# One stretch of fixed order from the second phase on, and attention's round in six steps

## The chip, the cores and the metric

The kernel runs on one core of one Trainium2 chip. The metric is the device time of one execution in microseconds, the median of several runs. TensorE (PE, with its weight loads as PEld), VectorE (DVE), ScalarE (ACT) and GpSimd (POOL) work beside each other; each takes its own instructions in order, and semaphores hold an instruction until its inputs are there and its output's buffer is free. SyncE (SP) issues all DMAs of this kernel, in one queue.

## The reference

Three layers follow each other on 4 x 768 = 3072 tokens of 256 values. A decayed linear attention (8 heads of 32 values, a state of 16 x 32 a head) goes over the sequence in chunks:

```
M = (C B^T) * exp(cum_i - cum_j), causal
y = M x + (C state) * exp(cum)
state = exp(sum) * state + sum_j B_j x_j * exp(cum_end - cum_j)
```

A first feed-forward layer takes `h = max(x w1, x w2, x w3)` (256 to 768) and `h w_out` (768 to 256); a second takes `h = x w_in` (256 to 2048), `g = max(h, 0) + alpha * min(h, 0)` and `g w_out`. The weights come as 64-bit floats.

## The kernel before

**Tiles.** The feed-forward layers run on six tiles of 512 tokens. Every operand is kept as two float32r halves, high and low, and a product is three matmuls (high by high, low by high, high by low). A unit of the first layer is 128 columns of `h`: three ups of six matmuls (`up<-xt,w`), ScalarE's copy `g<-up` of the first, VectorE's maximum with the two others, the halves `gh` (ScalarE) and `gl` (GpSimd, `halves`), and two units later a down of six matmuls (`acc<-gh,wo`, `acc<-gl,wo`). A unit of the second layer is one up of six (`up<-yt,vi`), two VectorE operations (a `TENSOR_SCALAR` and a `SCALAR_TENSOR_TENSOR` to `g`), the same halves, and a down with `vo`. `up` has 3 buffers of PSUM, `acc` 2, attention's `at` 3. At a layer's end `end1` writes `yt` from `acc` with ScalarE and VectorE.

**Phases.** PHASES lists (layer, tile): first layer on tile 0 (in two halves), first layer on tile 1, second layer on tile 0, first layer on tile 2, second layer on tile 1, and so on to two last phases of the second layer. The first layer has 6 units a tile, the second 16. In what follows the phases are counted from one; the second phase is the first layer on tile 1, from 83 us on, and the third the second layer on tile 0, from 121.7 us on. The two downs that are left of a phase are carried into the next (`carry`).

**Attention** goes block by block (24 blocks of 128 tokens, `r`), four blocks for each tile. Its steps are `load`, `att_a` (GpSimd: B and C times decays), `att_t` (transposes), `att_e` (exponentials on ScalarE, then the causal select on GpSimd), `att_b` (the product of C and B, `at<-bc` or `at<-st,v`, and VectorE's multiplication into `e`), `att_u` (the state), `att_y` (the output, `at<-cpt,u` and `at<-e,xm`, then `xt` by ScalarE and VectorE). From block 12 on (NDIR) the blocks are wide: `att_s` writes `tok`, VectorE transposes it to `ts`, `att_t` writes that to DRAM (`sc`), and `att_l` reads it back in eight DMAs to `v` and `st` buffers. `rounds` strings the steps together; a round is five of them. `quota` says how many steps are due after a unit, `attend` takes the next one.

**Weights.** 28 pieces of weights are converted on the way: a DMA to one of three `st` buffers, a re-bias on ScalarE (`st<-st`), a shift and an or on VectorE (`v<-st`, `v<-st,v`), a copy on ScalarE (`vi<-v`) and a subtract on VectorE (`vi<-v,vi`). `slot` and `quota_w` pace them.

**What sets the order.** In the first three phases the scheduler of the tile framework sets each engine's order. From `n_ph >= STRICT` (3, the fourth phase) on, every phase is a stretch in which instructions stand as they are written (`tc.manual_schedule`); there attention's steps are taken after an up and after a down.

Of the kernel before, what the change touches and what calls it, by code (L numbers as in the profile page):

```python
# [37 lines left out]

LEADW = 12288

STRICT = 3
AHEAD = 10
START = 4
LAG = 2
NX = 3

# [31 lines left out]
def fused(ctx: ExitStack, tc: tile.TileContext, x, a, B, C, w1, w2, w3, w_out, v_in, v_out, alpha, cst, out):  # L78
# [133 lines left out]
    def load(r):  # L212
        for q in (r, r + 1)[r > AHEAD:1 + (r >= AHEAD)]:
            load_bc(q)
        load_x(r)
# [210 lines left out]
        nc.scalar.activation(blk[r]["m"], src, AF.Exp)  # L426
        yield

    def att_e(r):
        b, k = divmod(r, NB)  # L430
        if r >= NDIR:
            for g in range(2):
                e = blk[r]["m", g]
                for q in range(4):
                    nc.scalar.activation(e[:, q, :], e[:, q, :], AF.Exp, bias=ncum[:, k, b, 4 * g + q:4 * g + q + 1])  # L435
                nc.gpsimd.affine_select(out=e, in_=e, pattern=[[0, 4], [1, P]], compare_op=ALU.is_ge, fill=0.0, base=0, channel_multiplier=-1)  # L436
            return
        e = blk[r]["m"]
        for h in range(H):
            nc.scalar.activation(e[:, h, :], e[:, h, :], AF.Exp, bias=ncum[:, k, b, h:h + 1])  # L440
        for c in range(2):
            m = e[c * Q:(c + 1) * Q]
            nc.gpsimd.affine_select(out=m, in_=m, pattern=[[0, H], [1, Q]], compare_op=ALU.is_ge, fill=0.0, base=0, channel_multiplier=-1)  # L443

# [112 lines left out]
    def rounds(r0):  # L557

        for r in range(r0, NR):
            if r + 2 < NR:  # L560
                yield lambda r=r: att_a(r + 2), 0
            yield lambda r=r: (att_y(r), r + 1 < NR and att_u(r + 1)), r + 1
            if r + 2 < NR:
                late = r + 2 == NDIR
                yield lambda r=r, late=late: (att_e(r + 1), late or att_s(r + 2)), 0
                yield lambda r=r, late=late: (att_b(r + 1), att_s(r + 2) if late else att_t(r + 2)), 0
                yield lambda r=r, late=late: (late and att_t(r + 2), load(r + 3), att_l(r + 2)), 0
            elif r + 1 < NR:
                yield lambda r=r: att_e(r + 1), 0
                yield lambda r=r: att_b(r + 1), 0  # L570

    todo = []
    y_done = [0]
# [53 lines left out]
    def halves(g, n, engine=nc.gpsimd):  # L627
# [2 lines left out]
        split(gh[:, :n], gl[:, :n], g, engine)  # L630
        return gh[:, :n], gl[:, :n]

    def up1(ph, f, o, n):
        t = ph[1]
        fs = slice(f * P, (f + 1) * P)
        g = un.tile([P, 512], F32, tag="g", name="g")[:, :n]
        for j in range(3):
            need(4 * (f // 2) + j)
            p = up_mm([w[:, j, :, fs] for w in w123], xt[t], o, n)
            if j == 0:  # L640
                nc.scalar.activation(g, p, AF.Copy)  # L641
            else:
                nc.vector.tensor_tensor(g, p, g, ALU.max)  # L643
            slot()
        return halves(g, n)

    def up2(ph, f, o, n):
        t = ph[1]
# [133 lines left out]
    if True:  # L782
# [10 lines left out]
        plan = [u for ph in PHASES for u in units_of(ph)]  # L793

        owed, at = 0.0, 0
        for n_ph, ph in enumerate(PHASES):
            with tc.manual_schedule() if n_ph >= STRICT else nullcontext():
                layer, t, _, pace = ph
                up, end = (up1, end1) if layer == 1 else (up2, end2)
                pend = []  # L800
                for f, o, n, _, blocks, _ in units_of(ph):
                    until(blocks)
                    owing[1] = pace or quota_w(at)
                    if n_ph >= STRICT and layer == 2 and len(pend) == 1:
                        carry.pop(0)()
                    pend.append((f, o, n, up(ph, f, o, n)))
                    owed += quota(at)
                    at += 1
                    while n_ph >= STRICT and owed > 0.999 and todo:
                        owed -= 1  # L810
                        attend()
                    if carry:
                        carry.pop(0)()
                    elif tail:
                        tail.pop(0)()
                    if len(pend) > LAG:
                        down(ph, *pend.pop(0))
                    slot()
                    if layer == 2:
                        slot()  # L820
                    while owed > 0.999 and todo:
                        owed -= 1
                        attend()
                for i, u in enumerate(pend):
                    def go(ph=ph, u=u, finish=end if i == LAG - 1 else None):
                        down(ph, *u)
                        if finish:
                            finish(ph)
                    carry.append(go)
        with tc.manual_schedule():  # L830
            for u in pend[:-1]:
                down(ph, *u)
            f, _, _, g = pend[-1]
            for o, n in LAST:
                down(ph, f, o, n, [x[:, o:o + n] for x in g])
                end2_last(ph, o, n)
                while tail:
                    tail.pop(0)()


_INS = ['x', 'a', 'B', 'C', 'moe_w1', 'moe_w2', 'moe_w3', 'moe_w_out', 'moe2_w_in', 'moe2_w_out', 'moe2_alpha']
# [22 lines left out]
```

## Time and profile before

| | us |
|---|---|
| runs: median of 3 | 553.9 |
| runs: lowest, highest | 553.26, 555.51 |
| the profiled execution | 553.52 |
| its span, first to last instruction | 551.8 |
| busy in the span: PE | 536.2 |
| busy: DVE, ACT, POOL | 330.5, 221.6, 235.0 |

The busy time of PE is modelled, since matmuls overlap: an engine at 97% may still wait. The chain of work that ended last is what sets the end, and the places where PE sat idle are what an order can change. The granted clock of TensorE is that of the full level (2.4 GHz) in every slice of the page.

### The profile page before, as it was taken

Reading aid. Unit: us, or ns where it says so; the run is one execution under the profiler, and the core shown is the slowest. Engines: PE = TensorE matmul, PEld = TensorE weight load, DVE = VectorE, ACT = ScalarE, POOL = GpSimd, SP = SyncE. Lnnn points to the kernel's source line nnn. Section 1 sums busy time; section 2 is a strip of 40 time slices with the busy share of each in tenths; the row PEclk is TensorE's granted clock in tenths of the full one; section 3 lists DMA queues with packets and bytes.
Section 4 is the critical chain, followed back from the end, with each engine's and each line's share of the span. In section 5 each row is a group of like instructions: output and inputs, shape, how many; then the busy total and the mean of one; then the engine's idle time right before and its main releaser. Section 6 shows DMA issues by size and latency. Waiting matters only on the chain.

```text
span 551.8 us, 9739 instructions
## 1 busy us (share of the span) xinstructions
PE 536.2 (97%) x3541; PEld 432.4 (78%) x3542; DVE 330.5 (60%) x587; ACT 221.6 (40%) x556; POOL 235.0 (43%) x256
## 2 busy tenths in 40 slices
PE   8888999999999999999999999999999999999996
PEld 4667888767878888788788788888777888888885
DVE  5887898986565446665446665446654326556553
ACT  5667687863232244244244244233342222222222
POOL 2143445454453245564235555333643214444441
PEclk9999999999999999999999999999999999999999
DMA  7978779731123853743773634743420200002001
GB/s 146 229 149 182 193 171 214 227 78 28 30 40 80 155 97 90 152 70 85 128 114 95 131 65 111 124 93 87 67 63 2 38 1 0 1 0 39 0 2 39
DMA packets 185632, 49.84 MB, mean 90 GB/s; under 512 B 144112, under 2 KB 177072, under 8 KB 185584
## 3 DMA queue, kind: packets, MB, share of 16 engines
q1 hardware_dynamic: 185584, 49.22, 42.4%
q8 instruction: 28, 0.46, 0.4%
q14 instruction: 20, 0.16, 0.1%
HBM read 40.48 MB, written 8.72 MB: 89 GB/s over the span
## 4 chain that ended last, share of the span: by engine, by line
PE 77%; DVE 7%; ACT 4%; DMA 4%; issue 3%; SPq 2%; POOL 1%; ACTq 0%; DVEq 0%; POOLq 0%
PE up L619 41%; PE acc L619 29%; DVE v L171 2%; PE at L523 1%; ACT e L440 1%; DMA st<-in_moe_w_out_dram 1%; DVE g L643 1%; PE at L452 1%; POOL gl L130 1%; DMA st<-in_moe_w_in_dram 1%; DMA e<-cum_w 1%; DMA e<-cum_d 1%; DVE e L467 1%; PE at L520 1%; ACT st L162 1%
## 5 line engine op out<-in xcount | busy, mean ns | idle before, releaser
L130 POOL TENSOR_TENSOR gl<-g,gh 128x512 fp32r<-128x512 f32 (+1 forms) x137 | 172.6, 1260 | 257.1 <-ACT gh L129 242.6
L129 ACT ACTIVATE gh<-g 128x512 fp32r<-128x512 f32 (+1 forms) x138 | 84.5, 612 | 261.7 <-DVE g L654 184.0
L619 PE MATMUL up<-xt,w 128*128 128x512 f32 (+1 forms) x756 | 161.5, 363 | 2.5 <-ACT g L641 1.7
L619 PEld LDWEIGHTS up<-xt,w 128*128 128x128 f32 x756 | 128.5, 188 | 27.6 <-ACT g L641 2.4
L619 PE MATMUL up<-yt,vi 128*128 128x512 f32 x576 | 146.0, 390 | 0.0
L619 PEld LDWEIGHTS up<-yt,vi 128*128 128x128 f32 x576 | 107.7, 188 | 23.0 <-issue 0.4
L653 DVE TENSOR_SCALAR g<-up,alph 128x512 f32<-128x512 f32 x96 | 71.8, 748 | 85.4 <-PE up L619 77.1
L619 PE MATMUL acc<-gh,vo 128*128 128x512 f32 (+1 forms) x392 | 120.5, 389 | 0.6 <-DVE yt L682 0.6
L643 DVE TENSOR_TENSOR g<-up,g 128x512 f32<-128x512 f32 (+1 forms) x84 | 51.4, 611 | 71.0 <-PE up L619 61.2
L619 PEld LDWEIGHTS acc<-gh,vo 128*128 128x128 f32 x392 | 72.1, 188 | 15.5 <-DVE yt L682 1.1
L619 PE MATMUL acc<-gl,vo 128*128 128x512 f32 (+1 forms) x196 | 76.0, 388 | 1.0 <-POOL gl L130 0.8
L654 DVE SCALAR_TENSOR_TENSOR g<-up,g 128x512 f32<-128x512 f32 x96 | 66.3, 691 | 3.3
L619 PE MATMUL acc<-gh,wo 128*128 128x512 f32 (+1 forms) x168 | 47.3, 366 | 0.2 <-ACT gh L129 0.2
L619 PEld LDWEIGHTS acc<-gl,vo 128*128 128x128 f32 x196 | 36.8, 188 | 9.9 <-POOL gl L130 2.1
L619 PEld LDWEIGHTS acc<-gh,wo 128*128 128x128 f32 x168 | 29.5, 189 | 5.7 <-ACT gh L129 0.4
L641 ACT ACTIVATE g<-up 128x512 f32<-128x512 f32 (+1 forms) x42 | 22.3, 532 | 26.2 <-PE up L619 15.9
L435 ACT ACTIVATE e<-e,ncum 128x128 f32<-128x128 f32 x96 | 29.6, 388 | 4.5 <-DMA e<-cum_w 4.5
L619 PE MATMUL acc<-gl,wo 128*128 128x512 f32 (+1 forms) x84 | 30.2, 360 | 0.0
L443 POOL TENSOR_SCALAR_AFFINE_SELECT e<-e 64x512 f32<-64x512 f32 x20 | 17.1, 856 | 14.9 <-ACT e L440 14.1
L440 ACT ACTIVATE e<-e,ncum 128x64 f32<-128x64 f32 x80 | 21.9, 341 | 2.3 <-DMA e<-cum_d 2.3
L171 DVE SCALAR_TENSOR_TENSOR v<-st,v 128x512 uint32<-128x512 uint32 x28 | 21.9, 783 | 0.9 <-ACT st L162 0.3
L454 DVE TENSOR_TENSOR e<-at,e 128x512 f32<-128x512 f32 x24 | 16.0, 686 | 10.4 <-POOL e L436 10.4
(123 smaller groups left out, 396.9 us busy)
## 6 DMA issues: line engine op xcount, KB each, us to landing
e<-cum_w SPq DMA_DIRECT2D x24, 256.0 KB, 4.4
st<-sc SPq DMA_DIRECT2D x48, 128.0 KB, 3.0
st<-in_moe_w_out_dram SPq DMA_DIRECT2D x11, 512.0 KB, 5.2
st<-in_moe_w_dram SPq DMA_DIRECT2D x9, 512.0 KB, 5.0
sc<-ts SPq DMA_DIRECT2D x40, 112.0 KB, 3.0
st<-in_moe_w_in_dram SPq DMA_DIRECT2D x8, 512.0 KB, 4.5
v<-sc SPq DMA_DIRECT2D x48, 64.0 KB, 2.8
out_dram<-st SPq DMA_DIRECT2D x22, 128.0 KB, 3.3
```

Of the source, the lines that this page charges most:

```text
L129: nc.scalar.activation(dst_h, src, AF.Copy)
L130: engine.tensor_tensor(dst_l, src, dst_h, ALU.subtract)
L171: nc.vector.scalar_tensor_tensor(v, hi, 3, v, ALU.logical_shift_left, ALU.bitwise_or)
L435: nc.scalar.activation(e[:, q, :], e[:, q, :], AF.Exp, bias=ncum[:, k, b, 4 * g + q:4 * g + q + 1])
L440: nc.scalar.activation(e[:, h, :], e[:, h, :], AF.Exp, bias=ncum[:, k, b, h:h + 1])
L443: nc.gpsimd.affine_select(out=m, in_=m, pattern=[[0, H], [1, Q]], compare_op=ALU.is_ge, fill=0.0, base=0, channel_multiplier=-1)
L454: nc.vector.tensor_tensor(ef, cb, ef, ALU.mult)
L619: nc.tensor.matmul(acc, w, r, start=(first and i == 0), stop=(last and i == len(todo_) - 1), skip_group_check=True)
L641: nc.scalar.activation(g, p, AF.Copy)
L643: nc.vector.tensor_tensor(g, p, g, ALU.max)
L653: nc.vector.tensor_scalar(g, p, 0.0, alph[:, f:f + 1], ALU.min, ALU.mult)
L654: nc.vector.scalar_tensor_tensor(g, p, 0.0, g, ALU.max, ALU.add)
```

## The change

- STRICT becomes 1: one single stretch of fixed order reaches from the second phase to the end, and only the first phase is left to the scheduler.
- In such phases the first layer's steps of attention are also handed out inside a unit, after its second up (`within`), and half of a unit's due steps count before the unit.
- From block 6 on (FINE) `rounds` calls `fine`, a round in six steps. The exponentials come in two halves (`att_e(r, part)`): the first half of block r + 2 at the end of round r, the second at the start of round r + 1, each with its select. `att_y`, `att_b`, `att_t` and `att_l` are steps of their own in wide blocks, and `att_l` stands ahead of `load`. In the one round where the wide blocks begin (`late`), the product of block 11 stands ahead of the output of block 10.
- AHEAD becomes 8 for 10: B and C are loaded a block ahead from block 8 on.
- The `gl` of the last unit of the first layer (not on tile 0) is made by VectorE.

```diff
-STRICT = 3
-AHEAD = 10
+STRICT = 1
+AHEAD = 8
+FINE = 6
...
-                yield lambda r=r, late=late: (late and att_t(r + 2), load(r + 3), att_l(r + 2)), 0
+                yield lambda r=r, late=late: (late and att_t(r + 2), att_l(r + 2), load(r + 3)), 0
...
+    def fine(r):
+        more, near = r + 2 < NR, r + 1 < NR
+        late = r + 2 == NDIR
+        if near:
+            yield lambda: (more and att_a(r + 2), att_e(r + 1, 1 if r > FINE else None)), 0
+        if late:
+            yield lambda: (att_b(r + 1), att_s(r + 2)), 0
+        yield lambda: (att_y(r), near and att_u(r + 1), more and not late and att_s(r + 2)), r + 1
+        if near and not late:
+            yield lambda: (att_b(r + 1), r + 2 < NDIR and att_t(r + 2)), 0
+        if more and r + 2 >= NDIR:
+            yield lambda: att_t(r + 2), 0
+            yield lambda: att_l(r + 2), 0
+        if more:
+            yield lambda: (load(r + 3), att_e(r + 2, 0)), 0
...
             slot()
-        return halves(g, n)
+            if j == 1 and within:
+                within[0]()
+        return halves(g, n, nc.vector if t and f == NF1 - 1 else nc.gpsimd)
...
-            with tc.manual_schedule() if n_ph >= STRICT else nullcontext():
...
+            if n_ph == STRICT:
+                fixed.enter_context(tc.manual_schedule())
+                within.append(hand_out)
...
+                own = quota(at)
+                if n_ph >= STRICT and layer == 1:
+                    owed += own / 2
+                    own /= 2
```

Three places of the new order follow. The first is VectorE in the middle of the second phase, where `v`, `vi` and `vo` belong to weights, `g<-up` to the feed-forward layer and `u`, `xt`, `e`, `bc` to attention. Before:

```order
L171 SCALAR_TENSOR_TENSOR v<-st,v 128x512
L169 TENSOR_SCALAR v<-st 128x512
L171 SCALAR_TENSOR_TENSOR v<-st,v 128x512
L554 TENSOR_TENSOR xt_1691<-at,xt_1690 128x128 x2
L501 TENSOR_TENSOR u<-at,ct 128x128
L177 TENSOR_TENSOR vi_114<-v,vi_113 128x2x256
L507 SCALAR_TENSOR_TENSOR u<-u,dec_f 128x64
L177 TENSOR_TENSOR vo_116<-v,vo_115 128x512
L507 SCALAR_TENSOR_TENSOR u<-u,dec_f 128x64
L169 TENSOR_SCALAR v<-st 128x512
L643 TENSOR_TENSOR g<-up,g 128x512
L171 SCALAR_TENSOR_TENSOR v<-st,v 128x512
```

Now:

```order
L171 TENSOR_SCALAR v<-st 128x512
L173 SCALAR_TENSOR_TENSOR v<-st,v 128x512
L666 TENSOR_TENSOR g<-up,g 128x512 x2
L179 TENSOR_TENSOR vo_116<-v,vo_115 128x512
L556 TENSOR_TENSOR xt_1630<-at,xt_1629 128x128 x2
L503 TENSOR_TENSOR u<-at,ct 128x128
L509 SCALAR_TENSOR_TENSOR u<-u,dec_f 128x64 x2
L171 TENSOR_SCALAR v<-st 128x512
L173 SCALAR_TENSOR_TENSOR v<-st,v 128x512
L666 TENSOR_TENSOR g<-up,g 128x512 x2
L179 TENSOR_TENSOR vi_114<-v,vi_113 128x2x256
L469 TENSOR_TENSOR e<-at,e 128x256 x2
```

Before, ten rows stand ahead of the next maximum `g`: attention's, and parts of four pieces of weights. Now six rows, with parts of two pieces, stand between two pairs of maxima.

The second is the start of the third phase on PE, where `up<-yt,vi` is the second layer, `acc<-gh,wo` a carried down of the first, and `at<-bc` the product of block 10 (before) or 11 (now). Before:

```order
L619 MATMUL up<-yt_1607,vi_113 128x512 x2
L619 MATMUL up<-yt_1607,vi_114 128x512 x2
L619 MATMUL up<-yt_1608,vi_113 128x512 x2
L619 MATMUL acc<-gh,vo_115 128x512
L619 MATMUL acc<-gh,vo_116 128x512
L619 MATMUL acc<-gl,vo_115 128x512
L619 MATMUL acc<-gh,vo_115 128x512
L619 MATMUL acc<-gh,vo_116 128x512
L619 MATMUL acc<-gl,vo_115 128x512
L462 MATMUL at<-bc 64x128 x8
```

Now:

```order
L640 MATMUL up<-yt_1667,vi_113 128x512 x2
L640 MATMUL up<-yt_1667,vi_114 128x512 x2
L640 MATMUL up<-yt_1668,vi_113 128x512 x2
L464 MATMUL at<-bc 64x128 x8
L640 MATMUL up<-yt_1667,vi_113 128x512 x2
L640 MATMUL up<-yt_1667,vi_114 128x512 x2
L640 MATMUL up<-yt_1668,vi_113 128x512 x2
L538 MATMUL at<-cpt,u 64x64 x8
L546 MATMUL at<-e,xm_106 32x64 x16
L497 MATMUL at<-xm_107,bp 32x128 x4
L640 MATMUL acc<-gh,vo_115 128x512
```

The first down of the second layer came right after the carried ones and one up; now two ups, the product of block 11 and the output of block 10 (`at<-cpt,u`, `at<-e,xm`) stand ahead of it. VectorE at the same place, before:

```order
L653 TENSOR_SCALAR g<-up,alph 128x512
L654 SCALAR_TENSOR_TENSOR g<-up,g 128x512
L682 TENSOR_TENSOR yt_1968<-acc,yt_1967 128x512 x2
L653 TENSOR_SCALAR g<-up,alph 128x512
L654 SCALAR_TENSOR_TENSOR g<-up,g 128x512
L467 TENSOR_TENSOR e<-at,e 128x256 x2
L393 TENSOR_TENSOR bc<-at,ct 128x256
L653 TENSOR_SCALAR g<-up,alph 128x512
```

Now:

```order
L678 TENSOR_SCALAR g<-up,alph 128x512
L679 SCALAR_TENSOR_TENSOR g<-up,g 128x512
L173 SCALAR_TENSOR_TENSOR v<-st,v 128x512
L707 TENSOR_TENSOR yt_2003<-acc,yt_2002 128x512 x2
L678 TENSOR_SCALAR g<-up,alph 128x512
L679 SCALAR_TENSOR_TENSOR g<-up,g 128x512
L179 TENSOR_TENSOR vi_114<-v,vi_113 128x2x256
L469 TENSOR_TENSOR e<-at,e 128x256 x2
L356 MEMSET tok 128x768
L171 TENSOR_SCALAR v<-st 128x512
```

A piece's rows (`v<-st,v`, `vi<-v,vi`) stand among the second layer's `g`, and the first `e` comes behind one of them.

The third is ScalarE in two rounds of wide blocks inside a phase of the second layer. Before:

```order
L129 ACTIVATE gh<-g 128x512
L435 ACTIVATE e<-e,ncum 128x128 x8
L363 ACTIVATE tok<-b 128x128
L364 ACTIVATE tok<-c 128x2x4x16
L129 ACTIVATE gh<-g 128x512 x5
L553 ACTIVATE xt_2634<-at 128x128 x2
L129 ACTIVATE gh<-g 128x512 x2
L435 ACTIVATE e<-e,ncum 128x128 x8
```

Now:

```order
L131 ACTIVATE gh<-g 128x512
L437 ACTIVATE e<-e,ncum 128x128 x4
L131 ACTIVATE gh<-g 128x512
L437 ACTIVATE e<-e,ncum 128x128 x4
L131 ACTIVATE gh<-g 128x512
L555 ACTIVATE xt_2555<-at 128x128 x2
L365 ACTIVATE tok<-b 128x128
L366 ACTIVATE tok<-c 128x2x4x16
```

Eight exponentials (`e<-e,ncum`) stood in one row; now they stand in two rows of four with a `gh` between, and the output's `xt` behind them.

## Rows read from the trace of the kernel before

**Rows 1.** The page: the chain that ended last, shares of the span by engine.

```profile
PE 77%; DVE 7%; ACT 4%; DMA 4%; issue 3%; SPq 2%; POOL 1%; ACTq 0%; DVEq 0%; POOLq 0%
```

**Rows 2.** Timeline of a steady stretch: start us, us, engine, line, operation [idle before].

```profile
147.08 1.52 PE L619 MATMUL up<-yt,vi 128*128 128x512 f32 x6
148.44 0.61 PE L619 MATMUL acc<-gh,vo 128*128 128x512 f32 x2
...
151.37 1.29 POOL L130 TENSOR_TENSOR gl<-g,gh 128x512 fp32r<-128x512 f32 x1 [1.83 <-PE up L619]
...
152.61 0.65 PE L462 MATMUL at<-bc 64*64 64x128 f32 x14
```

**Rows 3.** PE's waits from 83 us on: us in total, times, longest us.

```profile
PE acc L619 <- POOL gl L130: 0.8, 2, 0.4
...
PE at L452 <- DMA st<-sc: 0.4, 1, 0.4
```

**Rows 4.** Timeline, the end of the second phase, PE and ACT.

```profile
112.77 0.39 PE L619 MATMUL acc<-gl,wo 128*128 128x512 f32 x1
...
113.20 0.67 ACT L162 ACTIVATE st<-st 128x512 f32<-128x512 f32 x1 [0.36 <-DMA st<-in_moe_w_out_dram]
...
114.39 3.88 PE L619 MATMUL up<-xt,w 128*128 128x512 f32 x14 [1.24 <-ACT g L641]
...
119.03 0.62 PE L619 MATMUL acc<-gh,wo 128*128 128x512 f32 x2
```

**Rows 5.** Timeline, the start of the third phase, PE and DVE.

```profile
127.27 1.52 PE L619 MATMUL up<-yt,vi 128*128 128x512 f32 x6
...
128.68 1.29 DVE L682 TENSOR_TENSOR yt<-acc,yt 128x512 fp32r<-128x512 f32 x2 [1.02 <-ACT yt L681]
...
129.43 0.73 PE L619 MATMUL acc<-gh,vo 128*128 128x512 f32 x2 [0.63 <-DVE yt L682]
```

**Rows 6.** Timeline at 222 us, DVE and PE.

```profile
216.76 0.69 DVE L454 TENSOR_TENSOR e<-at,e 128x512 f32<-128x512 f32 x1 [1.34 <-POOL e L436]
...
222.37 0.61 PE L619 MATMUL acc<-gh,vo 128*128 128x512 f32 x2
...
223.40 0.50 PE L619 MATMUL acc<-gl,vo 128*128 128x512 f32 x1 [0.42 <-POOL gl L130]
...
223.74 0.62 PE L619 MATMUL acc<-gh,vo 128*128 128x512 f32 x2
```

**Rows 7.** Stretches: length, then busy (instructions) of PE, PEld, DVE, ACT, POOL; clock; DMA.

```profile
83.00:121.70 38.70, 37.34 (x297) 28.95 (x295) 33.96 (x61) 29.66 (x75) 20.73 (x20) 1.00 0.70 180
121.70:168.50 46.80, 46.17 (x332) 36.68 (x329) 29.52 (x52) 13.57 (x32) 22.01 (x23) 1.00 0.23 41
```

**Rows 8.** Groups in the second phase, then the third: shapes xcount | busy us, mean ns | idle.

```profile
L171 DVE SCALAR_TENSOR_TENSOR v<-st,v 128x512 uint32<-128x512 uint32 x11 | 8.4, 760 | 0.4 <-ACT st L162 0.3
...
L169 DVE TENSOR_SCALAR v<-st 128x512 uint32<-128x512 uint32 x10 | 6.0, 596 | 0.9 <-DMA st<-in_moe_w_in_dram 0.9
...
L177 DVE TENSOR_TENSOR vo<-v,vo 128x512 fp32r<-128x512 f32 x6 | 4.4, 742 | 1.4 <-ACT vo L175 1.3
...
L467 DVE TENSOR_TENSOR e<-at,e 128x256 f32<-128x256 f32 x4 | 1.5, 410 | 0.0
...
L130 POOL TENSOR_TENSOR gl<-g,gh 128x512 fp32r<-128x512 f32 x6 | 9.5, 1579 | 8.0 <-ACT gh L129 7.9
...
L130 POOL TENSOR_TENSOR gl<-g,gh 128x512 fp32r<-128x512 f32 x15 | 19.3, 1290 | 21.3 <-ACT gh L129 17.8 <-PE up L619 1.8 <-PE at L544 1.4
...
L653 DVE TENSOR_SCALAR g<-up,alph 128x512 f32<-128x512 f32 x15 | 11.2, 749 | 11.8 <-PE up L619 11.6
```

**Rows 9.** Timeline, an output of the first layer's phases, PE and DVE.

```profile
270.64 0.64 PE L523 MATMUL at<-e,xm 128*32 128x128 f32 x16
...
271.93 0.49 DVE L554 TENSOR_TENSOR xt<-at,xt 128x128 fp32r<-128x128 f32 x2 [0.86 <-ACT xt L553]
```

**Rows 10.** PE's waits from 20 to 83 us.

```profile
PE at L462 <- DVE xt L554: 1.1, 1, 1.1
```

More of the change, by code (lines that the diff above doesn't have):

```diff
@@ L427, in first_e, with att_e @@
         yield
-    def att_e(r):
+    def att_e(r, part=None):
         b, k = divmod(r, NB)
         if r >= NDIR:
-            for g in range(2):
+            for g in range(2) if part is None else (part,):
                 e = blk[r]["m", g]
@@ L438, in att_e @@
         e = blk[r]["m"]
-        for h in range(H):
+        for h in range(4 * (part or 0), 4 if part == 0 else H):
             nc.scalar.activation(e[:, h, :], e[:, h, :], AF.Exp, bias=ncum[:, k, b, h:h + 1])
-        for c in range(2):
+        for c in range(0 if part == 0 else 2):
             m = e[c * Q:(c + 1) * Q]
@@ L559, in rounds @@
         for r in range(r0, NR):
+            if r >= FINE:
+                yield from fine(r)
+                continue
             if r + 2 < NR:
@@ L631, in halves @@
         return gh[:, :n], gl[:, :n]
+    within = []
     def up1(ph, f, o, n):
@@ L795, in fused @@
         owed, at = 0.0, 0
-        for n_ph, ph in enumerate(PHASES):
-            with tc.manual_schedule() if n_ph >= STRICT else nullcontext():
[L798 to L817, printed above, removed]
-                    slot()
[L819 to L838, printed above, removed]
+        fixed = ExitStack()
+        def hand_out():
+            nonlocal owed
+            while owed > 0.999 and todo:
+                owed -= 1
+                attend()
@@ new lines, in fused, with go @@
+        for n_ph, ph in enumerate(PHASES):
+            if n_ph == STRICT:
+                fixed.enter_context(tc.manual_schedule())
+                within.append(hand_out)
+            layer, t, _, pace = ph
+            up, end = (up1, end1) if layer == 1 else (up2, end2)
+            pend = []
+            for f, o, n, _, blocks, _ in units_of(ph):
+                until(blocks)
+                owing[1] = pace or quota_w(at)
+                own = quota(at)
+                if n_ph >= STRICT and layer == 1:
+                    owed += own / 2
+                    own /= 2
+                if n_ph >= STRICT and layer == 2 and len(pend) == 1:
+                    carry.pop(0)()
+                pend.append((f, o, n, up(ph, f, o, n)))
+                owed += own
+                at += 1
+                if n_ph >= STRICT:
+                    hand_out()
+                if carry:
+                    carry.pop(0)()
+                elif tail:
+                    tail.pop(0)()
+                if len(pend) > LAG:
+                    down(ph, *pend.pop(0))
+                slot()
+                if layer == 2:
+                    slot()
+                hand_out()
+            for i, u in enumerate(pend):
+                def go(ph=ph, u=u, finish=end if i == LAG - 1 else None):
+                    down(ph, *u)
+                    if finish:
+                        finish(ph)
+                carry.append(go)
@@ L841 @@
+        for u in pend[:-1]:
+            down(ph, *u)
+        f, _, _, g = pend[-1]
+        for o, n in LAST:
+            down(ph, f, o, n, [x[:, o:o + n] for x in g])
+            end2_last(ph, o, n)
+            while tail:
+                tail.pop(0)()
+        fixed.close()
 _INS = ['x', 'a', 'B', 'C', 'moe_w1', 'moe_w2', 'moe_w3', 'moe_w_out', 'moe2_w_in', 'moe2_w_out', 'moe2_alpha']
```

## The prediction

> **What bounds the kernel now.** I read the chain of work first: three quarters of it is PE, so PE's own row of matmuls sets the end, and other engines matter only where they make PE wait [rows 1]. Then the steady stretch of the second layer: six matmuls of 512 columns start every 1.36 us (147.08 to 148.44), 0.227 us each, and a 512-column feed-forward matmul cannot come sooner anywhere in this kernel [rows 2]. The change adds and takes away no matmul, and PE has 33 groups of attention matmuls between feed-forward ones from the second phase on, where it had 34 (one moves ahead into the first phase). So PE's work stands, and only its waits can go or come.
>
> The list of PE's waits from 83 us on, where the second phase begins, is short [rows 3], and each place is seen in the timeline. Times below are from start to start, less 0.227 us a matmul; after each stop the first matmul also takes 0.11 us longer.
> - Second phase, 112.77 to 119.03 us: 1.62 - 0.23 = 1.39 us, in which PE waits for ScalarE's copy `g`, queued behind a `st` that waits for a weight's DMA; then 18 matmuls take 4.64 us where 18 x 0.227 = 4.08, 0.56 more. Together 1.95 us [rows 4].
> - Border to the third phase: the first `acc<-gh,vo` starts 2.16 us after six matmuls began that need 1.36: 0.80 us, waiting for VectorE's `yt` [rows 5].
> - Two equal places (222 and 306 us) of 0.58 + 0.11 us: `gl` comes late, since VectorE's queue stood 1.34 us at `e`, waiting for GpSimd's select after eight exponentials in a row [rows 6]. Together 1.38 us.
> - One wait of 0.43 us for `st<-sc` (389 us) [rows 3].
> The sum is 1.95 + 0.80 + 1.38 + 0.43 = 4.56 us. That is all there is to gain after the first phase.
>
> **Weights spread out.** In the second phase VectorE is busy 34.0 of 38.7 us and in the next 29.5 of 46.8 [rows 7]. The crowd is the conversion of weights: 11 pieces, each 0.60 + 0.76 + 0.74 = 2.1 us on VectorE [rows 8]. By the new order 5 stand in the second phase and 6 in the third, so 6 x 2.1 = 12.6 us move: 34.0 becomes 21.4 of 38.7, and 29.5 becomes 42.1 of 46.8. Each piece is also issued with its DMA two to three pieces ahead, at a piece in a unit of 24 x 0.227 = 5.4 us instead of one in 38.7 / 11 = 3.5, so `st` on ScalarE no longer meets a DMA in flight. I count the 1.95 us as gone. What is late next there is PE itself: VectorE has 17 us to spare.
>
> **The border and the exponentials.** The last unit's `gl` goes to VectorE (some 0.74 us, as the subtract of a piece, which has the same size, against GpSimd's 1.29 us [rows 8]), both trailing downs are put ahead of the next up, and two ups and the attention work lie between them and the first `acc<-gh,vo`: some 5 us where `yt` needs 1.29 [rows 5]. The 0.80 us go. With the exponentials done in halves, two steps ahead of the product that reads them, VectorE finds the select done: the 1.38 us go. The reads `st<-sc` get a step of their own right behind the transposes and ahead of the loads, a whole round before their matmul: the 0.43 us go. On SP these eight reads pass three loads, which are wanted a round later; nobody waits for those.
>
> **What it adds.** (1) At the start of the third phase the product of block 11 stands before block 10's output, one up apart (the PE rows of the change). Both take two of the three `at` buffers, so the second half of the output must wait until VectorE's first `e` has read the product. From the end of the last trailing down: `yt` needs about 0.8 for PE's tail and ScalarE's first copy (its second half is ready as soon as VectorE is) and 1.29 on VectorE, `g` of the next up 2 x 0.75 (its second operation taken as long as the first), the `vi` piece 0.74, the first `e` 0.41: 4.7 us [rows 5, 8]. PE comes there after an up, eight pairs and an up: 1.36 + 0.65 + 1.36 = 3.4 us [rows 2]. I take 4.7 - 3.4 = 1.3, with the piece's copy ahead of `yt` on ScalarE 1.5 us, plus 0.11 us: 1.6 us. Bounds: 0, if `yt` and the piece come a unit sooner, and 2.5 us, if two steps of VectorE also meet GpSimd's `gl`. Queued behind it on PE are only downs, whose halves are ready.
> (2) The six pieces in the third phase push `gl` back. In the steady stretch the `gl` of the up at 147.08 us ends at 152.66 [rows 2]. It is the third matmul of the down that stands five sixes later: 147.08 + 5 x 1.36 + 2 x 0.227 = 154.33, so 1.7 us of slack. A shift and an or of one piece are 1.36 us, which fits; with a product (2 x 0.41) or a transpose behind it, it does not. Two or three of 12 units are so placed; half a wait of 0.69 us [rows 6] is 0.35 us, bounds 0 and 6 x 0.69 = 4.1 us.
> GpSimd's own durations speak to this: `gl` takes 1.58 us among conversions and 1.29 without [rows 8]. The Trainium skill (SBUF — State Buffer, "Who interferes with whom") says that a VectorE instruction with two SBUF inputs and a GpSimd instruction that reads SBUF shut each other out for a whole instruction; the rows agree. By the row 0.29 us comes off a slack of 1.7 and the sum stands; by the rule's worst, a whole `or` and a whole `subtract` in the way of one `gl`, 1.5 us come off it, and every piece costs a wait. By the row the sum is 550.9, by the rule 554.6, the rival B below.
> (3) In three places later on the product follows the output by only six matmuls. There `xt` is done 1.78 us after the output's first matmul with `e` (270.64 to 272.42), and the product comes 0.64 + 1.36 = 2.0 us after it [rows 9]: no wait, with 0.2 us to spare; at most three waits of 0.4.
> (4) In the first phase the scheduler now sees that phase alone: a pair of pieces fewer is drawn into it, a product more. PE's order there is nearly the same. I take 0; bounds -1.1 and +1.1 us, the largest single wait there [rows 10].
>
> **The sum**, against the profiled execution (553.5 us, span 551.8): 553.5 - 4.56 + 1.6 + 0.35 = 550.9 us. The median of the runs is 553.9, 0.4 above it; their spread is 2.2 us.
>
> **The rivals.**
> A, the forecast: 550.9, between 549.3 (no wait of kind 1) and 552.5. Chance 0.50.
> B, the conversions bite in the third phase: VectorE and GpSimd take turns, and each of six pieces costs one wait of 0.69 us: 553.5 - 4.56 + 1.6 + 4.1 = 554.6. For it: VectorE at 42 of 47 us, crowded into 12 of 16 units, and `gl` at 1.58. Against it: the second phase had 11 pieces in 38.7 us and lost 1.95 us. Chance 0.22.
> C, slower, by one transfer: block 12's reads `st<-sc` take a place in the ring of three `st` buffers that the weights use. They wait in SP's order for the write of `sc` and for a piece to be read, and the last weight's DMA stands behind all eight of them. If that weight comes more than four units late (4 x 2.72 = 11 us), PE stands at the second layer's fifteenth unit until the last two pieces are through. When pieces came as fast as they could, one took 38.7 / 11 = 3.5 us [rows 7, 8], so two are 7.0 us: 553.5 - 4.56 + 1.6 + 7.0 = 557.5. Against it: the reads are due some seven units after the transposes, and the last weight is asked for eight units before it is needed. Chance 0.10.
> D, more gain: no wait at the product, and the first phase loses its 1.1 us [rows 10]: 553.5 - 4.56 - 1.1 = 547.8. Chance 0.10.
> E, the waits only move (a `gl` or `yt` late at another border, since every clump still has the same length on its engine): 553.5. Chance 0.08.
>
> **How the numbers follow.** The likeliest is A, 550.9. About 0.5% is what a measurement of this kernel can tell from no change; of 553.9 that is a line at 551.1, which runs through A. Of A 0.31 lies below the line and 0.19 above; D is below; B and E are no change, with 0.02 of them below; C is slower, and 0.01 of B. So faster 0.43, same 0.46, slower 0.11. The range leaves out C and half of D: 548.5 to 555.0.
>
> **What would show it.** Right: no wait of PE between 83 us and the third phase; VectorE near 21 us of the second phase and 42 of the third; no wait at `e` for a select; one stop of PE at `at<-cpt,u` or `at<-e,xm` early in the third phase, released by VectorE's `e`. B shows as several stops at `acc<-gl,vo` in the third phase, with `gl` near 1.6 us; C as one long stop at an `up` or `acc` there, released by a weight. I am wrong altogether if the first phase ends at another time by more than 1 us, since nothing here prices the scheduler's choice.

## The result, and the profile after

The changed kernel takes 548.88 us, the median of 4 runs (547.77 to 550.39), beside 554.7 us for the kernel before (4 runs, 553.26 to 556.06). The ratio is 0.9898, 95% interval 0.9867 to 0.9930: faster by 1.0%, or 5.8 us by the medians. A later series gave 0.9891 (0.9860 to 0.9921). The forecast was 550.9 us, range 548.5 to 555.0, with "no change" slightly likelier than "faster". So the direction and the range held, with the median 0.4 us inside the range's lower end. It lies below 549.3 us, the lower end of the likeliest case, A, and above D's 547.8: the gain is larger than the 2.6 us that I had summed.

The profiled executions are closer together than the medians: 553.52 us before and 548.96 after, 4.56 us apart (spans 551.8 and 547.2). The page of the changed kernel: busy time by engine, and the chain that ended last by engine.

```profile
PE 536.1 (98%) x3541; PEld 434.4 (79%) x3542; DVE 333.0 (61%) x592; ACT 223.1 (41%) x556; POOL 224.9 (41%) x251
...
PE 87%; DMA 4%; DVE 3%; ACT 3%; issue 1%; SPq 1%; POOL 0%; ACTq 0%; DVEq 0%; POOLq 0%
```

PE is as busy as before, and its share of the chain went from 77% [rows 1] to 87%: the same work, fewer waits. The list of PE's waits from 83 us on, which answers [rows 3]:

```profile
PE at L386 <- DVE xt L556: 0.6, 1, 0.6
PE at L538 <- DVE e L469: 0.4, 1, 0.4
PE up L732 <- ACT v L723: 0.2, 1, 0.2
PE acc L640 <- DVE gl L132: 0.2, 1, 0.2
```

None of the four places that the prediction listed is left. The first row ends at 83.70 us, 0.3 us before the second phase's first up, and belongs to the first phase; the last two stand at the end of the kernel, as before. What is new is `at<-cpt,u` waiting for VectorE's `e`, at the place that the prediction named. The stretches, the second and most of the third phase, answer [rows 7] (same columns):

```profile
83.00:120.70 37.70, 37.14 (x305) 29.59 (x298) 27.09 (x52) 23.09 (x63) 13.69 (x17) 1.00 0.56 140
120.70:167.00 46.30, 45.86 (x315) 36.76 (x314) 41.12 (x68) 22.42 (x52) 24.52 (x25) 1.00 0.45 103
```

**Three stretches of PE.** The end of the first phase differs by some 3 us between kernels whose first phase has the same instructions in the same order, but from there on a kernel repeats itself: the changed kernel, profiled twice, took 85.47 and 85.50 us, then 374.16 and 374.16. So I compare three lengths, read from the timeline by PE's starts: to the first 512-column up (the first phase's end), from there to the fourth phase's first up (second and third phase), and from there to the last matmul.

| kernel | first phase ends | second + third | fourth on |
|---|---|---|---|
| before | 83.05 | 87.95 | 376.89 |
| changed | 84.00 | 85.47 | 374.16 |
| changed, again | 83.99 | 85.50 | 374.16 |
| order_only | 83.21 | 84.87 | 376.06 |
| rounds_only | 84.73 | 85.88 | 374.16 |
| late_undone | 87.17 | 85.91 | 374.17 |
| gl_pool | 84.09 | 85.62 | 374.18 |
| exp_whole | 83.54 | 85.81 | 374.16 |
| exp_late | 85.68 | 90.01 | 374.16 |
| dve_more | 84.24 | 90.46 | 374.16 |
| fine11 | 83.79 | 94.35 | 374.16 |
| reads_old | 83.13 | 84.86 | 376.16 |
| ahead_only | 85.57 | 84.87 | 374.68 |
| one_stretch | 82.65 | 88.47 | 376.29 |

Where the new round starts at block 6 (changed, rounds_only, late_undone, gl_pool, exp_whole, exp_late, dve_more) two pieces of PE's work stand in an earlier column: one product with its transposes (0.90 us, 126.69 to 127.59 in order_only) in the first, and four `at<-st,v` (0.47 us, 153.67 to 154.14 in the changed kernel) in the second; fine11 has only the latter. With equal work the changed kernel gains 87.95 - (85.47 + 0.90 - 0.47) = 2.05 us in the second and third phase, 376.89 - (374.16 + 0.47) = 2.26 us from the fourth on, and in the first 83.05 - (84.00 - 0.90) = -0.05 us. The sum is 4.26 us, as the last matmul shows (547.89 to 543.63); 0.3 us more lies behind it, in the last outputs.

### The profile page after: what moved, and what is told of

Its sections match the earlier page's. It is cut to its first block, busy times and chain, and to the rows that moved or that the text cites. A ratio compares the mean times of both kernels' runs of the same rounds, so it can differ in the third digit from the quotient of the medians.

```text
span 547.2 us, 9715 instructions
## 1 busy us (share of the span) xinstructions
PE 536.1 (98%) x3541; PEld 434.4 (79%) x3542; DVE 333.0 (61%) x592; ACT 223.1 (41%) x556; POOL 224.9 (41%) x251
## 4 chain that ended last, share of the span: by engine, by line
PE 87%; DMA 4%; DVE 3%; ACT 3%; issue 1%; SPq 1%; POOL 0%; ACTq 0%; DVEq 0%; POOLq 0%
PE up L640 48%; PE acc L640 31%; PE at L525 1%; DMA st<-in_moe_w_out_dram 1%; PE at L454 1%; DMA e<-cum_d 1%; DMA b<-in_B_dram 1%; DMA st<-in_moe_w_in_dram 1%; PE at L546 1%; PE at L464 1%; ACT e L442 1%; PE at L522 1%; PE up L750 1%; PE at L538 1%; DVE v L173 0%
## 5 line engine op out<-in xcount | busy, mean ns | idle before, releaser
L132 POOL TENSOR_TENSOR gl<-g,gh 128x512 fp32r<-128x512 f32 (+1 forms) x132 | 165.2, 1252 | 252.3 <-ACT gh L131 243.5
L173 DVE SCALAR_TENSOR_TENSOR v<-st,v 128x512 uint32<-128x512 uint32 x28 | 23.4, 836 | 2.7 <-ACT st L164 1.4
L445 POOL TENSOR_SCALAR_AFFINE_SELECT e<-e 64x512 f32<-64x512 f32 x20 | 14.4, 722 | 17.7 <-ACT e L442 17.0
L164 ACT ACTIVATE st<-st 128x512 f32<-128x512 f32 x28 | 19.0, 677 | 4.5 <-DMA st<-in_moe_w_in_dram 2.1
```

The lines of the kernel that those rows point to most:

```text
L132: engine.tensor_tensor(dst_l, src, dst_h, ALU.subtract)
L164: nc.scalar.activation(hi, hi, AF.Prelu, scale=2.0 ** -112, alpha=2.0 ** 32)
L173: nc.vector.scalar_tensor_tensor(v, hi, 3, v, ALU.logical_shift_left, ALU.bitwise_or)
```

## The experiments

### Each half of the change alone

order_only: the fixed order, without the new round.

```diff
-FINE = 6
-AHEAD = 8
+FINE = 24
+AHEAD = 10
```

> The fixed order from the second phase on, alone: rounds stay as they were (FINE = 24, so no fine round; AHEAD = 10). My theory: the stops of the second phase (1.95 us) and of its border (0.80 us) go, the two late gl (1.38 us) and the late read of st (0.43 us) stay, and since the round that begins the wide blocks puts block 10's output ahead of block 11's product, the new stop of 0.58 us is not there. Profiled execution 553.5 - 2.75 = 550.8 us. Rival: the stops of the second phase went because the exponentials in halves relieve ScalarE there; then this kernel still shows them and stays at 553.5 us or above.

Measured: ratio 0.9911 (0.9879 to 0.9942), and PE's waits from 83 to 540 us are one row:

```profile
PE acc L640 <- POOL gl L132: 0.8, 2, 0.4
```

These are the two late `gl` (now at 220 and 304 us). The second and third phase are 3.08 us shorter, more than the 2.75 expected, and the wait for `st` at 389 us is gone too, which I had put down to the new round. order_only also hands out attention's steps inside a unit (`within`); whether the single stretch or this hand-out cures the second phase was not run apart.

rounds_only: the new round, with the scheduler for the second and third phase.

```diff
-STRICT = 1
+STRICT = 3
```

> The round in six steps alone: STRICT = 3 again, so the scheduler orders the second and third phase. My theory: 1.38 + 0.43 = 1.81 us go, the stops of the second phase and its border (2.75 us) stay, 551.7 us; together with the fixed order alone this makes the whole 4.56 us. Rival: the two halves need each other, and this one gains under 0.8 us or loses, since the scheduler puts the new steps in another order in the second phase.

Measured: ratio 0.9889 (0.9844 to 0.9934). From the fourth phase on it is the changed kernel to 0.01 us: 2.26 us of gain, where I had said 1.81. The scheduler's second phase takes 38.25 us (84.73 to 122.98) against 36.70 in the changed kernel and 38.63 before, but the stop at the border went here too: the scheduler now puts two ups ahead of the first `acc<-gh,vo`. By equal work the second and third phase gain 87.95 - (85.88 + 0.43) = 1.64 us. So the halves do not add: 3.9 us and 3.9 us (1.64 + 2.26), together 4.3. Most of the second phase's 1.9 us needs order_only's part (0.4 of it came here too), the two late `gl` need the new round, or one move of it (ahead_only, below), and the border and the read at 389 us are had from either.

### The stop at the first wide round

late_undone:

```diff
-        if late:
-            yield lambda: (att_b(r + 1), att_s(r + 2)), 0
         yield lambda: (att_y(r), ... more and not late and att_s(r + 2)), r + 1
-        if near and not late:
-            yield lambda: (att_b(r + 1), r + 2 < NDIR and att_t(r + 2)), 0
+        if near:
+            yield lambda: (att_b(r + 1), late and att_s(r + 2), r + 2 < NDIR and att_t(r + 2)), 0
```

> The whole change, but in the round where the wide blocks begin, block 10's output stands ahead of block 11's product again. My theory: the stop of 0.58 us at the second half of the output early in the third phase was made by the product in two of the three at buffers, and goes: 549.0 - 0.6 = 548.4 us, no stop between 121 and 132 us. Rival: the second half of the output comes too early for something else as well (the state or the select of block 10), and a stop of 0.4 us or more stays there, or the product now waits for xt by as much: 549.0 us.

Measured: ratio 0.9919 (0.9883 to 0.9955); second and third phase 0.44 us longer, not 0.6 shorter. The stop at the output is gone and two others came, of 0.61 and 0.40 us. Timeline (start us, us, engine, line, operation, idle before and its releaser):

```profile
132.06 0.42 ACT L555 ACTIVATE xt<-at 128x128 fp32r<-128x128 f32 x2
...
132.35 0.49 DVE L556 TENSOR_TENSOR xt<-at,xt 128x128 fp32r<-128x128 f32 x2 [0.32 <-ACT xt L555]
...
132.69 0.85 PE L464 MATMUL at<-bc 64*64 64x128 f32 x16 [0.44 <-DVE xt L556]
...
143.84 1.47 POOL L132 TENSOR_TENSOR gl<-g,gh 128x512 fp32r<-128x512 f32 x1 [2.76 <-ACT gh L131]
...
145.36 0.50 PE L638 MATMUL acc<-gl,vo 128*128 128x512 f32 x1 [0.24 <-POOL gl L132]
```

The product now comes one up behind the output and waits for `xt`. Output and product share three buffers, and in these two orders whichever goes second waits for VectorE. It is not so everywhere: order_only has no wait there at all. My rival was right.

gl_pool:

```diff
-        return halves(g, n, nc.vector if t and f == NF1 - 1 else nc.gpsimd)
+        return halves(g, n, nc.gpsimd)
```

> The whole change, but the gl of the first layer's last unit is made by GpSimd again. What I said in the prediction: this edit helps the border, so 0.6 us (1.29 less 0.70) come back at the start of the third phase. What the profile of the changed kernel says: the gl done at 121.63 us is first read at 123.88 us, 2.25 us later, so 0.6 us more is hidden, no stop appears at any border, and the time stays at 549.0 us.

Measured: ratio 0.9901 (0.9874 to 0.9928), 85.62 us: 0.15 more, and all of it is that the stop at the output went from 0.58 to 0.72 us. No border stops. Neither number was right: the engine of `gl` does nothing for the border, as the slack of 2.25 us said, and `e` comes 0.13 us later for it: GpSimd's select, now behind that `gl`, lies beside VectorE's `v<-st,v` (0.82 us for 0.68), and ScalarE's and VectorE's rows follow later.

### Exponentials: in halves, or ahead?

exp_whole has them two steps ahead, in one row of eight; exp_late in halves, one step ahead.

The first:

```diff
-            yield lambda: (more and att_a(r + 2), att_e(r + 1, 1 if r > FINE else None)), 0
+            yield lambda: (more and att_a(r + 2), r == FINE and att_e(r + 1)), 0
...
-            yield lambda: (load(r + 3), att_e(r + 2, 0)), 0
+            yield lambda: (load(r + 3), att_e(r + 2)), 0
```

The second:

```diff
-            yield lambda: (more and att_a(r + 2), att_e(r + 1, 1 if r > FINE else None)), 0
+            yield lambda: (more and att_a(r + 2), att_e(r + 1, 0)), 0
...
-            yield lambda: (att_b(r + 1), att_s(r + 2)), 0
+            yield lambda: (att_e(r + 1, 1), att_b(r + 1), att_s(r + 2)), 0
-        yield lambda: (att_y(r), ... att_s(r + 2)), r + 1
+        yield lambda: (att_y(r), ... att_s(r + 2), near and not late and att_e(r + 1, 1)), r + 1
...
-            yield lambda: (load(r + 3), att_e(r + 2, 0)), 0
+            yield lambda: load(r + 3), 0
```

> The whole change, but all eight exponentials of block r + 2 at the end of round r, in one row: two steps ahead, not in halves. Theory: what mattered is that they are ahead, so VectorE's e finds the select done, no stop at 222 and 306 us, and from the fourth phase's first up to the last matmul it takes 374.2 us as in the changed kernel. Rival: a row of eight (8 x 0.39 = 3.1 us) on ScalarE pushes gh, and with it gl, past its slack of 1.2 to 2.5 us in places: stops of 0.5 us or more, 375.2 us or above.

> The whole change, but the halves of block r + 1's exponentials stand in round r, the first ahead of the step of the output, the second behind it, a step ahead of the product: in halves, but not two steps ahead. Theory: being ahead is what mattered, so VectorE's e meets an unfinished select again, and stops of 0.3 us or more come up from the fourth phase on: 374.8 us or above. Rival: halves alone are enough, 374.2 us.

Measured: both take 374.16 us from the fourth phase on. So a whole row two steps ahead is enough, and so are halves one step ahead in a round of six steps. Whether the halves or the six steps do it in the second case is open, since a whole row one step ahead was not run in that round. For exp_late my theory missed there. What it did show is in the third phase, in the one round where its second half stands in the product's own step:

```profile
130.11 0.45 PE L538 MATMUL at<-cpt,u 32*64 32x64 f32 x8
130.59 1.05 ACT L442 ACTIVATE e<-e,ncum 128x64 f32<-128x64 f32 x4
130.76 1.26 POOL L132 TENSOR_TENSOR gl<-g,gh 128x512 fp32r<-128x512 f32 x1 [3.16 <-DMA e<-cum_w]
131.98 1.38 POOL L445 TENSOR_SCALAR_AFFINE_SELECT e<-e 64x512 f32<-64x512 f32 x2
133.39 0.76 DVE L469 TENSOR_TENSOR e<-at,e 128x256 f32<-128x256 f32 x2 [2.83 <-POOL e L445]
...
133.86 0.45 PE L538 MATMUL at<-cpt,u 32*64 32x64 f32 x8 [3.31 <-DVE e L469]
```

`e` waits for the select, the select stands behind these four exponentials (done at 131.64) and a `gl` (done at 132.02), and PE stands 3.5 us (start to start) at the output. With the clock's fall behind it, the second and third phase took 4.5 us longer than the changed kernel's.

### How near the rival B was

dve_more:

```diff
-            nc.vector.tensor_tensor(l, v, h, ALU.subtract)
+            for _ in range(2 if i >= 22 else 1):
+                nc.vector.tensor_tensor(l, v, h, ALU.subtract)
```

> The whole change, but the subtract of each of the last six pieces is done twice, 0.7 us more of VectorE for each, in the third phase (it writes the same values again). It tells how near the changed kernel is to the rival B. In the changed kernel the smallest slacks of gl in the third phase are 0.05, 0.66 and 0.86 us. If B is as near as that, two to four stops at acc<-gl come up there, together 1 to 2 us (85.5 us from the second to the fourth phase become 86.5 to 87.5). Rival: GpSimd's gl is not behind these subtracts, and nothing but the stop at the output grows by 0.7 us, to 86.2 us.

Measured: 90.46 us, 5.0 us more than the changed kernel, for 6 x 0.7 = 4.2 us of VectorE's work. Its waits of PE from 83 us on:

```profile
PE acc L641 <- POOL gl L132: 2.2, 4, 0.7
PE at L539 <- DVE e L470: 1.1, 1, 1.1
PE acc L641 <- ACT gh L131: 0.8, 1, 0.8
```

The stop at the output grew by 0.73 us (0.58 to 1.31) and five stops of 0.46 to 1.0 us came at `acc`. That is more than either side had said. In the changed kernel the third phase has no room for one more subtract a piece. The list of slacks (from a `gl`'s end to the matmul that reads it) did not tell where: the four `gl` that came late had 0.86, 2.48, 1.18 and 0.05 us in the changed kernel, and the one with 0.66 us held. The share does point that way: VectorE's 41.1 of 46.3 us become 45.3 with 4.2 us more, and in dve_more it hardly paused between the output at 154 us and the last stops, 15.78 us busy of 16.06 (columns as in [rows 7]):

```profile
154.14:170.20 16.06, 14.31 (x62) 10.60 (x60) 15.78 (x24) 4.89 (x10) 7.28 (x7) 1.00 0.26 49
```

I read this as a delay of VectorE that carries over from one unit into the next; no run separates that from the subtract and `gl` keeping each other out (below).

### The read at 389 us

reads_old: order_only, with the reads behind the loads as in the kernel before.

```diff
-                yield lambda r=r, late=late: (late and att_t(r + 2), att_l(r + 2), load(r + 3)), 0
+                yield lambda r=r, late=late: (late and att_t(r + 2), load(r + 3), att_l(r + 2)), 0
```

> The fixed order alone, and the reads st<-sc behind the loads again as in the kernel before (FINE = 24, AHEAD = 10, att_l after load). With the reads ahead of the loads, that kernel had no stop at 389 us and took 376.06 us from the fourth phase's first up to the last matmul, the kernel before 376.89. Theory: this one line is the 0.43 to 0.6 us: the stop at at<-st,v comes back, 376.6 us. Rival: the stop went because attention's steps stand at other places in the unit now, and it stays at 376.1 us.

Measured: no stop, 376.16 us. My theory fell. What held the reads shows in SP's queue in the kernel before:

```profile
369.14 2.42 SPq L379 DMA_DIRECT2D sc<-ts  x4
371.61 0.80 SPq L235 DMA_DIRECT2D xm<-in_x_dram  x1
381.05 1.15 SPq L329 DMA_DIRECT2D e<-cum_w  x2
382.38 0.37 SPq L402 DMA_DIRECT2D cpt<-sc  x1
382.80 0.43 SPq L407 DMA_DIRECT2D v<-sc  x1
```

A load of `e<-cum_w` waited 8.6 us for PE's output to free its buffer, and the reads stood behind it: 13.2 us after the write of `sc`, where every other wide block but the first has them 4.3 to 6.4 us after it. In the program the reads are written first. The border between two stretches of fixed order lies between, and the order came out turned there. one_stretch tests that: the kernel before, with its later stretches joined into one.

```diff
-            with tc.manual_schedule() if n_ph >= STRICT else nullcontext():
...
+            if n_ph == STRICT:
+                fixed.enter_context(tc.manual_schedule())
```

> The kernel before with one thing changed: the stretches of fixed order of the fourth and later phases, one for each phase, are one single stretch (the scheduler still orders the first three phases, the rounds, the loads and gl are as before). In the kernel before, the queue of SP stands 8.6 us at e<-cum_w, which waits for PE's output to free its buffer, and the reads of sc, written earlier in the program, stand behind it since the border between two stretches lies there. Theory: with one stretch the reads stand ahead of e<-cum_w again and the stop at 389 us goes: 376.89 - 0.6 = 376.3 us from the fourth phase's first up to the last matmul, the two late gl still there, and the stops of the second and third phase as before: about 553 us. Rival: the reads are late for another reason, and it stays at 376.9 us.

Measured: 376.29 us, as expected (553.05 us in its one run). The queue at that place:

```profile
371.80 0.78 SPq L237 DMA_DIRECT2D xm<-in_x_dram  x1
374.10 0.34 SPq L404 DMA_DIRECT2D cpt<-sc  x1
...
381.23 0.94 SPq L331 DMA_DIRECT2D e<-cum_w  x2
```

So 0.6 us of the gain come from joining the stretches. (Its second and third phase, ordered by the scheduler from the same text as before, came out 0.5 us longer.)

### Two tries at a faster kernel

fine11: old rounds up to block 10, the new one from block 11 on.

```diff
-AHEAD = 8
-FINE = 6
+AHEAD = 10
+FINE = 11
```

> The fixed order from the second phase on, with the old rounds up to block 10 and the round in six steps from block 11 on (FINE = 11, AHEAD = 10). The kernel with the fixed order alone needs 84.87 us from the first 512-column up of the second phase to the first up of the fourth phase, the changed kernel needs 374.16 us from there to the last matmul. Theory: the two add, 84.9 + 374.2 = 459.1 us, where the changed kernel has 459.63 with 1 us of PE's work less in it (a product done in the first phase) and the fixed order alone has 460.93. With a first phase that ends at 83.2 us: 542.3 us to the last matmul, about 547.6 us. Rival: the change of rounds at block 11 makes a stop of its own in the third phase or leaves the select of block 12 late, 0.6 us or more.

Measured: ratio 1.0033 (1.0007 to 1.0059); 556.95 us, with 9.0 us lost in the third phase (94.35 us against 84.87 + 0.47 of moved work), some 2 us of them by a lower clock (last section). SP's queue:

```profile
150.57 2.14 SPq L381 DMA_DIRECT2D sc<-ts  x4
155.99 0.30 SPq L409 DMA_DIRECT2D v<-sc  x1
...
159.24 0.44 SPq L411 DMA_DIRECT2D st<-sc  x1
159.77 0.40 SPq L227 DMA_DIRECT2D b<-in_B_dram  x1
```

PE at the same time:

```profile
155.02 1.54 PE L640 MATMUL up<-yt,vi 128*128 128x512 f32 x6
163.23 1.19 PE L454 MATMUL at<-st,v 128*128 128x256 f32 x4 [6.67 <-DMA b<-in_B_dram]
```

PE comes to block 12's product at 156.4 us, when SP has only begun to issue its reads. From the first read to the product it takes 7.2 us here with PE waiting; the changed kernel has 12.5 us between them (141.13 to 153.67), order_only 8.05. The profile names another DMA, `b`, as releaser; `b` was issued right behind the last `st<-sc`, and the product reads only the latter. It is not the branch `late` that makes this room: late_undone, without it, has 12.9 us between the two. What does was not tried; fine11 differs from the changed kernel by AHEAD and by the block at which the new round starts.

ahead_only: order_only, and of the new round only the exponentials, whole, at the end of the round before.

```diff
-                yield lambda r=r, late=late: (att_e(r + 1), late or att_s(r + 2)), 0
+                yield lambda r=r, late=late: (r <= NDIR - 1 and att_e(r + 1), late or att_s(r + 2)), 0
...
-                yield lambda r=r, late=late: (late and att_t(r + 2), att_l(r + 2), load(r + 3)), 0
+                yield lambda r=r, late=late: (late and att_t(r + 2), att_l(r + 2), load(r + 3), r >= NDIR - 1 and att_e(r + 2)), 0
...
-                yield lambda r=r: att_e(r + 1), 0
```

> The fixed order from the second phase on with the old rounds (FINE = 24, AHEAD = 10), and of the new round only this: from block 13 on, the eight exponentials stand whole at the end of the round before, after the loads, instead of a step ahead of the product. Theory: that one move is the rest of the gain. No stop at 220 and 304 us; from the fourth phase's first up to the last matmul 376.06 - 1.9 = 374.2 us as in the changed kernel; second and third phase 84.9 us as with the fixed order alone, without the stop of 0.58 us at the output; a first phase with one product less, ending near 83.2 us. Last matmul at 542.3 us, 1.3 us before the changed kernel's; about 547.5 us against its 548.9. Rival: the old round has one step less, so a row of eight exponentials falls next to gh more often and gl comes late, 0.5 us or more at two places or more: no faster than the changed kernel.

> The changed kernel itself again, beside the one before it on the same chip. From the second phase on, every matmul should stand where it stood (459.6 us from the first 512-column up of the second phase to the last matmul, within 0.1 us); what differs from run to run is the end of the first phase, 84.0 us in the first profile and 84 to 87 us in kernels with the same first phase.

Measured: no wait of PE from 86 to 540 us; by equal work 85.90 - 84.87 = 1.0 us less than the changed kernel in the second and third phase, and the same from the fourth on (374.68 against 374.63). But 549.63 us (546.98 to 551.77, ratio 0.9899, 0.9864 to 0.9933) beside 548.81 (547.79 to 550.15) for the changed kernel: not told apart. In its profile the first phase ended at 85.57 us, with a stop of 1.8 us at 38.6 us that its neighbours lack. I don't call it faster. What it shows is that the exponentials' place alone is worth the late `gl`: 376.06 - 374.68 = 1.38 us.

## Why the prediction came out as it did

- **Second phase, 1.95 us:** right. 38.63 us became 36.70 with the same matmuls. Its means was right too (one stretch of order, pieces spread), but VectorE's time was not: I said 21.4 us, it is 27.1. The pieces' rows did go down by 12.2 us (23.4 to 11.2; I said 12.6). But I had taken the rest as fixed, and it grew by 3.7 us, most of it attention's (six `e` stand there now for four [rows 8]). And rows overlap, by 3.8 us in the 34.0 of before and 2.1 us now, so 1.7 us of what I took off had been no busy time of its own. It cost nothing, as PE does not wait for VectorE there.
- **Border, 0.80 us:** gone, by the order (two ups between). The part on `gl` was wrong: gl_pool shows no stop with GpSimd.
- **Late `gl`, 1.38 us:** right, by the place of the exponentials. "In halves, two steps ahead" is one condition more than needed: two steps ahead does it in one row.
- **`st<-sc`, 0.43 us:** gone, but for another reason than I gave. It was no matter of three loads, but of one DMA waiting for its buffer at the border of two stretches. I had read the wait of PE and not SP's queue behind it. Its size was also too small: start to start it was 0.82 - 0.23 = 0.60 us.
- **(1) The new stop:** the mechanism and the place were right, the size was not, 0.58 us for 1.6. The changed kernel at the start of the third phase:

```profile
124.78 1.52 PE L640 MATMUL up<-yt,vi 128*128 128x512 f32 x6
...
124.99 1.07 ACT L706 ACTIVATE yt<-acc 128x512 fp32r<-128x512 f32 x2
125.60 1.29 DVE L707 TENSOR_TENSOR yt<-acc,yt 128x512 fp32r<-128x512 f32 x2 [1.18 <-ACT yt L706]
...
126.83 1.65 PE L640 MATMUL up<-yt,vi 128*128 128x512 f32 x6
...
128.19 0.68 DVE L179 TENSOR_TENSOR vi<-v,vi 128x512 fp32r<-128x512 f32 x1
...
128.41 0.45 PE L538 MATMUL at<-cpt,u 32*64 32x64 f32 x8
128.79 0.75 DVE L469 TENSOR_TENSOR e<-at,e 128x256 f32<-128x256 f32 x2
...
129.26 0.45 PE L538 MATMUL at<-cpt,u 32*64 32x64 f32 x8 [0.40 <-DVE e L469]
```

  From the last down's end (124.78) VectorE's first `e` was done after 4.4 us (128.79 + 0.38), not 4.7, and the copy ahead of `yt` on ScalarE cost nothing (`yt` began 0.2 us after the down). PE came after 3.63 us, not 3.4, and then ran the output's first half, 0.24 us, which needs no `e`. So 0.3, 0.2, 0.23 and 0.24 us, all on one side, make the 1.0 us. The output's first half I had left out; the other three I had taken for the worse.
- **(2) `gl` in the third phase, 0.35 us:** about right; one `gl` came late, by 0.2 us, at 165.70 us. Two others were done 0.66 and 0.86 us ahead. The rows show VectorE and GpSimd in each other's way:

```profile
136.72 0.65 DVE L179 TENSOR_TENSOR vo<-v,vo 128x512 fp32r<-128x512 f32 x1
136.74 1.79 POOL L132 TENSOR_TENSOR gl<-g,gh 128x512 fp32r<-128x512 f32 x1 [2.62 <-ACT gh L131]
...
160.30 1.30 POOL L132 TENSOR_TENSOR gl<-g,gh 128x512 fp32r<-128x512 f32 x1 [2.77 <-ACT gh L131]
160.48 1.67 DVE L179 TENSOR_TENSOR vo<-v,vo 128x512 fp32r<-128x512 f32 x1
```

  When the subtract began first, `gl` took 0.5 us more than its 1.29; when `gl` began first, the subtract took 1.0 us more than its 0.68 and ended 0.55 us after `gl`. The Trainium skill (SBUF — State Buffer, "Who interferes with whom") says that a VectorE instruction with two SBUF inputs contends with a GpSimd instruction that reads SBUF, by an exclusive lock, and that issue order decides which of them waits. The trace agrees on the order, and nearly on the lock: if nothing overlapped, this `gl` would take 1.92 us and this subtract 1.80, each 0.13 us more than measured. B did not come, but dve_more shows that 0.7 us a piece lay between.
- **(3) The product behind the output, no wait:** right, none of it in the list of waits.
- **(4) First phase, 0:** right as far as can be told, and within 0.1 us in this pair by luck. Six profiles have the first phase of before (it ends at 82.65 to 85.57 us, median 83.17), eight the new one with one product more (83.54 to 87.17, median 84.17). Less 0.90 us for the product, the medians lie 0.10 us apart, but the two kinds spread by 2.9 and 3.6 us, each with one order of instructions. Part of that seems to be the clock. In this pair it fell in the changed kernel alone (columns as in [rows 7]; before, then now):

```profile
44.00:48.00 4.00, 3.54 (x38) 3.19 (x37) 2.49 (x8) 3.10 (x11) 1.02 (x2) 1.00 0.87 172
```

```profile
44.00:48.00 4.00, 4.00 (x33) 3.67 (x30) 2.06 (x6) 3.09 (x11) 1.41 (x3) 0.60 0.80 147
```

  The latest end of either kind goes with the most of it: 0.50 in the same stretch in ahead_only (85.57 us); 0.69 there and 0.65 from 76 to 80 us in late_undone (87.17 us). It is not the whole, since gl_pool kept 1.00 and ended at 84.09 us, the changed kernel at 84.00. What else makes the spread was not tried.
- **The total:** 2.6 us forecast, 4.3 us by PE's starts: 1.0 from (1), 0.2 from (2), 0.2 from the stop at 389 us. Some 0.3 us from the fourth phase on (2.26 - 1.38 - 0.60) has no cause that I know. The runs' 5.8 us and the profiles' 4.6 lie within one interval (3.9 to 7.4 us).

## What to carry to other kernels

Read the queue behind a wait before naming its cause: PE's wait at 389 us named a DMA of `sc`, and the cure was to free SP's queue of one load that waited for its buffer. Before putting more work on an engine, look both at how long ahead of its reader each hand-over is done and at how much the engine still pauses: in dve_more, where VectorE hardly paused, a slack of 2.48 us was used up too. And where a first part of the kernel varies from run to run, compare fixed stretches after it, matmul start to matmul start with equal work; two profiles of one kernel agreed within 0.03 us there.

## What was new about the hardware

A long stop costs more than its length. After PE's 6.8 us stop in fine11 the granted clock was 0.54 over the next 4.7 us (columns as in [rows 7]):

```profile
140.00:156.00 16.00, 16.00 (x135) 12.68 (x134) 13.73 (x23) 10.32 (x28) 11.29 (x12) 1.00 0.26 59
163.30:168.00 4.70, 4.70 (x14) 3.88 (x15) 1.89 (x3) 0.00 (x0) 0.00 (x0) 0.54 0.46 120
168.00:173.00 5.00, 5.00 (x24) 4.10 (x23) 2.80 (x4) 0.63 (x1) 1.29 (x1) 1.00 0.00 0
```

A matmul of 512 columns then started every 0.427 us, against 0.227 before and after: the 1.2 GHz level, some 2 us lost on top of the stop. After the 3.5 us stop of exp_late the clock was 0.61 from 134 to 138 us. The stops of up to 1.3 us in dve_more's third phase left the clock there at 1.00. But the length of one stop does not decide it alone. In the first phase PE stood 0.95 us at 41.6 us in the changed kernel, and 0.95 us at 41.7 us in the kernel before; the clock then fell to 0.60 (44 to 48 us) in the one and stayed at 1.00 in the other. What makes the difference was not tried.
